# Splitting a down-projection weight over partitions: 13 rows each and a remainder on four load engines, instead of 12 rows and five small pieces

## The chip, the cores and the metric

The kernel runs on one core of a Trainium2 chip. The metric is device time in microseconds (us) of one execution. It reads about 95 MB from HBM once and does little arithmetic on each byte.

## The reference

One decode step for a batch of B = 2 with one token each, D = 512, all in float32. The output is the input plus an attention block plus a gated feed-forward block, both on the layer-normalised input:

```python
def _A_ref(x, k_cache, v_cache, wq, wo):     # Hq = 32 heads of Dh = 128, Hkv = 8
    W = min(4096, max(256, Sk // 4))         # 4096: the last W cached positions
    q = (x @ wq).reshape(B, Sq, Hq, Dh)...
    scores = einsum("bhqd,bhkd->bhqk", q, k) * (Dh ** -0.5)
    o = einsum("bhqk,bhkd->bhqd", softmax(scores), v)
    return o.reshape(B, Sq, Hq * Dh) @ wo    # wo: 4096 x 512

def _B_ref(x, W_gate, W_up, W_down):         # F = 1792
    gate = einsum("bsd,df->bsf", x, W_gate)
    up = einsum("bsd,df->bsf", x, W_up)
    gate = gate * (gate > 0)
    return einsum("bsf,fd->bsd", gate * up, W_down)   # W_down: 1792 x 512

xn = _layernorm(x)
return x + _A_ref(xn, ...) + _B_ref(xn, ...)
```

## The kernel before

All large transfers are issued by SP in program order into a pool `ring` of four buffers of 32 KB per partition, so a transfer is issued when the buffer four places earlier has been read. The order is: `wq` (two halves of 4 MB), `W_gate` and `W_up` (3.5 MB each), then for four groups of (key/value head quad, batch row) two `k` tiles and, one group later, two `v` tiles of 4 MB, then `W_down` (3.5 MB, `load_down`), then `wo` in two halves of 4 MB, the second cut into pieces of 8, 5, 2 and 1 rows per partition so that little is left to do when the last one lands.

PE runs in the order in which the code is written. After the query projection comes the gated unit: `g_ps` and `u_ps` hold gate and up in a layout of four groups of 32 partitions (each group takes a quarter of the 1792 columns, 448), one element per column. ScalarE and VectorE make `hh` = relu(gate) * up from them, and small matmuls against columns of the identity (`ht_ps`) turn `hh` so that the feed-forward index runs over partitions; `hT` holds the result. Then, for each `k` tile, 64 blocks are transposed (`pk`, copied to `kT` by VectorE and ScalarE in turn), multiplied by the queries (`scores`), and, one group later, the softmax weights are multiplied with `v` (`values`, `o`). At the end, `project` adds `hT` times `W_down` and the attention output `oT` times `wo` into one accumulator `y_ps`, four matmuls for each row of the weight in a partition.

Row k of a partition of `W_down` has to meet the element of `hT` at the same partition and k. With 1792 = 128 x 14 rows, a plain split would give 14 rows a partition. `load_down` uses another one: the 1792 rows are 32 runs of 56, and of each run the first 48 go to four partitions with 12 rows each (one transfer, 24 KB per partition), the last 8 to four partitions with two rows each. These remainders go in five small transfers, with 4 KB per partition: three of 8 runs (32 partitions each), and two of 4 runs (16 partitions each), the last into a tile of its own, `wx`. One part of the `W_down` tile is cleared by GpSimd first.

Of the kernel before, what the change touches and what calls it, by code (L numbers as in the profile page):

```python
# [9 lines left out]
F32 = mybir.dt.float32  # L10
AF = mybir.ActivationFunctionType
ALU = mybir.AluOpType
# [8 lines left out]
def kernel(  # L21
# [12 lines left out]
    nc = tc.nc  # L34
    P = 128
    B, _, D = x.shape
# [3 lines left out]
    F = w_gate.shape[1]  # L40
    W = min(4096, max(256, SK // 4))
    KC = D // P
# [3 lines left out]
    Q = 4  # L46
# [6 lines left out]
    PK = P // 2  # L53
    J = W // PK
    FB = F // P
    FQ = F // Q
    assert (B, REP, DH, S1, J) == (2, 4, P, 2, 64)

    const = ctx.enter_context(tc.tile_pool(name="const", bufs=1))
    ring = ctx.enter_context(tc.tile_pool(name="ring", bufs=RING))  # L60
    ktp = ctx.enter_context(tc.tile_pool(name="ktp", bufs=2))
    work = ctx.enter_context(tc.tile_pool(name="work", bufs=2))
    ps_kt = ctx.enter_context(tc.tile_pool(name="ps_kt", bufs=3, space=PSUM))
    ps_s = ctx.enter_context(tc.tile_pool(name="ps_s", bufs=1, space=PSUM))
    ps_1 = ctx.enter_context(tc.tile_pool(name="ps_1", bufs=1, space=PSUM))
# [13 lines left out]
    def load_ff(w, name):  # L79
        return load(name, w.rearrange("(p k) f -> p k f", p=P), [P, KC, F])  # L80
# [3 lines left out]

    FR = F // 32
    FM = FB - 2
    assert FR == 4 * FM + 8
    wx = const.tile([16, 2, D], F32, name="wx")  # L90

    def load_down():
        t = ring.tile([P, FM + 4, D], F32, name="wd", tag="ring")
        runs = w_down.rearrange("(i x) e -> i x e", i=32)
        main = bass.AP(
            tensor=w_down.tensor, offset=w_down.offset, ap=[[FR * D, 32], [FM * D, 4], [1, FM * D]]
        )
        nc.sync.dma_start(t[:, 0:FM].rearrange("p k e -> p (k e)"), main)
        nc.gpsimd.memset(t[32:64, FM + 2:], 0.0)
        for i, n, dst in (  # L100
            (0, 8, t[0:32, FM:FM + 2]), (8, 8, t[32:64, FM:FM + 2]), (16, 8, t[0:32, FM + 2:]),
            (24, 4, t[32:48, FM + 2:]), (28, 4, wx),
        ):
            src = runs[i:i + n, 4 * FM:, :].rearrange("i (y s) e -> i y (s e)", s=2)
            nc.sync.dma_start(dst.rearrange("p s e -> p (s e)"), src)
        return t

    def load_kv(cache, name, g, a):
        r, b = divmod(g, B)
        base = cache[b, r * C + 2 * a, SK - W:SK, :]  # L110
        run = J * DH
        src = bass.AP(
            tensor=cache.tensor, offset=base.offset, ap=[[run, PK], [SK * DH, 2], [1, run]]
        )
        return load(f"{name}{g}_{a}", src, [P, run])
# [15 lines left out]
    ident = const.tile([P, P], F32, name="ident")  # L131
# [7 lines left out]
    eps_t = const.tile([32, 1], F32, name="eps_t")  # L139
    nc.vector.memset(eps_t, EPS)  # L140

    hT = const.tile([P, FM + 6, B, 16], F32, name="hT")
    nc.gpsimd.memset(hT, 0.0)
    oT = const.tile([P, R, NJ, B, 16], F32, name="oT")
    nc.gpsimd.memset(oT, 0.0)
    xsel = const.tile([B, B, 16], F32, name="xsel")
# [53 lines left out]
    for kc in range(KC):  # L200
        m, k = divmod(kc, 2)
        for o, cols in ((0, xn.rearrange("r (m p k) -> r m k p", m=2, k=2)[:, m, k]), (1, xn.rearrange("r (p k) -> r k p", k=KC)[:, kc])):
            nc.tensor.matmul(xt_ps[:, o, kc, :], cols, rep.rearrange("r s b -> r (s b)"), start=True, stop=True)  # L203
    xnT = const.tile([P, 2, KC, 32], F32, name="xnT")
# [4 lines left out]
    for kc in range(KC):  # L209
        for r in range(R):  # L210
            for c in range(C):
                n = r * C + c
                nc.tensor.matmul(  # L213
                    q_ps[r][32 * c:32 * c + 32, :], xnT[:, 0, kc, :], wqt[kc // 2][:, kc % 2, n * 512:(n + 1) * 512],
                    start=(kc == 0), stop=(kc == KC - 1),
                )
    gw = load_ff(w_gate, "wg")
    uw = load_ff(w_up, "wu")
    for r in range(R):
        qs = work.tile([P, 512], F32, name=f"qs{r}", tag="qs")  # L220
# [6 lines left out]
        for b in range(B):  # L227
            dst = qz[:, r * B + b].rearrange("p (a s h k) -> p a s h k", a=NP, s=S1, h=2)
# [3 lines left out]
                )  # L232


    g_ps = ps_kt.tile([P, FQ], F32, name="g_ps", tag="kt")
    u_ps = ps_kt.tile([P, FQ], F32, name="u_ps", tag="kt")
    for dst, wt in ((g_ps, gw), (u_ps, uw)):
        for kc in range(KC):
            for c in range(Q):
                nc.tensor.matmul(  # L240
                    dst[32 * c:32 * c + 32, :], xnT[:, 1, kc, :], wt[:, kc, c * FQ:(c + 1) * FQ],
                    start=(kc == 0), stop=(kc == KC - 1),
                )
    gs = work.tile([P, FQ], F32, name="gs", tag="qs")
    nc.scalar.copy(gs, g_ps)
    gr = work.tile([P, FQ], F32, name="gr", tag="qs")
    nc.vector.scalar_tensor_tensor(gr, gs, 0.0, gs, op0=ALU.is_gt, op1=ALU.mult)
    hh = work.tile([P, FB, 32], F32, name="hh", tag="qs")
    gv = gr.rearrange("p (i x) -> p i x", i=8)
    uv = u_ps.rearrange("p (i x) -> p i x", i=8)  # L250
    nc.vector.tensor_tensor(
        hh[:, 0:FM].rearrange("p k (i y) -> p i y k", i=8), gv[:, :, 0:4 * FM].rearrange("p i (y k) -> p i y k", y=4),
        uv[:, :, 0:4 * FM].rearrange("p i (y k) -> p i y k", y=4), op=ALU.mult,
    )
    nc.vector.tensor_tensor(
        hh[:, FM:].rearrange("p s (i y) -> p i y s", i=8),
        gv[:, :, 4 * FM:].rearrange("p i (y s) -> p i y s", s=2),
        uv[:, :, 4 * FM:].rearrange("p i (y s) -> p i y s", s=2), op=ALU.mult,
    )
    ht_ps = ps_1.tile([P, FM + 6, B], F32, name="ht_ps", tag="misc")  # L260
    for k in range(FM):
        for c in range(Q):
            nc.tensor.matmul(
                ht_ps[32 * c:32 * c + 32, k], hh[:, k], ident[:, 32 * c:32 * c + B], start=True, stop=True
            )
    for s in range(2):
        for c, p0, k, cols in ((0, 0, 0, (0, 32)), (1, 32, 0, (0, 32)), (2, 0, 2, (0, 32)), (3, 32, 2, (0, 16)), (3, 0, 4, (16, 32))):
            nc.tensor.matmul(
                ht_ps[p0:p0 + cols[1] - cols[0], FM + k + s], hh[:, FM + s, cols[0]:cols[1]],
                ident[:, 32 * c:32 * c + B], start=True, stop=True,  # L270
            )
    for n, lo, hi in ((P, 0, FM), (64, FM, FM + 2)):
        nc.vector.tensor_copy(hT[0:n, lo:hi, :, 0], ht_ps[0:n, lo:hi])
    for p0, n, lo, hi in ((0, 32, FM + 2, FM + 4), (32, 16, FM + 2, FM + 4), (0, 16, FM + 4, FM + 6)):
        nc.vector.tensor_copy(hT[p0:p0 + n, lo:hi, :, 0], ht_ps[p0:p0 + n, lo:hi])

# [115 lines left out]
    def finish(g):  # L394
        r, b = divmod(g, B)
        if b == 0:
            osb[r] = const.tile([HR, B, P], F32, name=f"osb{r}")
        nc.vector.tensor_scalar(osb[r][:, b], oa[g], rls[g], 2.0, op0=ALU.mult, op1=ALU.mult)

    def spread_heads(r):  # L400
        op = ps_1.tile([P, NJ, B], F32, name=f"op{r}", tag="misc")
        for e in range(NE):
            nc.tensor.matmul(  # L403
                op, spread[:, e].rearrange("h k e -> h (k e)"),
                osb[r][:, :, e * NJ:(e + 1) * NJ].rearrange("h b j -> h j b"),
                start=(e == 0), stop=(e == NE - 1),
            )
        nc.vector.tensor_copy(oT[:, r, :, :, 0], op)
# [33 lines left out]
    g = NG - 1  # L442
    scores(*pend.pop())
    vin = [load_kv(v_cache, "v", g, a) for a in range(NP)]
    dw = load_down()
    for _ in softmax(g):
        pass

# [9 lines left out]
    def project(lhsT, w, stop):  # L458
        for e in range(Q):
            nc.tensor.matmul(  # L460
                y_ps[32 * e:32 * e + 17, :], lhsT.rearrange("p b s -> p (b s)")[:, 0:17],
                w[:, e * P:(e + 1) * P], start=False, stop=stop,
            )
# [2 lines left out]
        values(g, a, vin[a])  # L466
        gather(g, a)
    finish(g)
    for k in range(FM + 4):
        n = P if k < FM else 64  # L470
        project(hT[0:n, k], dw[0:n, k], False)
    for k in range(2):
        project(hT[0:16, FM + 4 + k], wx[:, k], False)
    spread_heads(R - 1)
    for r, cuts in ((0, (0, NJ)), (1, (0, 8, 13, 15, NJ))):
        wt = ring.tile([P, NJ, D], F32, name=f"wo{r}", tag="ring")
# [35 lines left out]
```

## Time and profile before

| | us |
|---|---|
| median of 3 runs | 231.94 (231.25 to 231.98) |
| profiled execution: its own span, first to last instruction | 230.3 |
| what lies around the span, against the median | 1.6 |
| PE busy in the span | 184.4 (80%) |
| VectorE busy | 67.1 (29%) |
| ScalarE busy | 48.4 (21%) |
| GpSimd busy | 6.6 (3%) |
| bytes moved by DMA | 95.15 MB in 3936 packets, 413 GB/s on average |

The page divides the span into 40 slices and shows in tenths how busy each engine was in each; the DMA row there is the mean over the core's 16 DMA engines. A transfer that SP issues is split by partitions over some or all of these 16 engines, each of which works through its own share in order; a transfer has landed when the slowest has written its share. In the queue rows, q1 is the queue of SP's transfers, and q8 brings the program's own instructions. The chain of waits is followed back from the last instruction, and shows at each step what the step had waited for.

### The profile page before, as it was taken

Reading aid. Unit: us, or ns where it says so; the run is one execution under the profiler, and the core shown is the slowest. Engines: PE = TensorE matmul, PEld = TensorE weight load, DVE = VectorE, ACT = ScalarE, POOL = GpSimd, SP = SyncE. Lnnn points to the kernel's source line nnn. Section 1 sums busy time; section 2 is a strip of 40 time slices with the busy share of each in tenths; the row PEclk is TensorE's granted clock in tenths of the full one; section 3 lists DMA queues with packets and bytes.
Section 4 is the critical chain, followed back from the end, with each engine's and each line's share of the span. In section 5 each row is a group of like instructions: output and inputs, shape, how many; then the busy total and the mean of one; then the engine's idle time right before and its main releaser. Section 6 shows DMA issues by size and latency. Waiting matters only on the chain.

```text
span 230.3 us, 4141 instructions
## 1 busy us (share of the span) xinstructions
PE 184.4 (80%) x1872; PEld 112.3 (49%) x1872; DVE 67.1 (29%) x136; ACT 48.4 (21%) x81; POOL 6.6 (3%) x23
## 2 busy tenths in 40 slices
PE   0295960849999889998999799589999974979593
PEld 0251220239666573664584565338566522148482
DVE  0500021023544462441472341147234123010000
ACT  2000100003444461540252331025133102000000
POOL 8100000000000000000000000000000100000000
PEclk9999799575999999999999999979999997699889
DMA  7999999999999999999999999999999999999980
GB/s 274 450 433 411 443 423 455 410 427 447 438 407 433 448 427 404 441 438 427 413 450 425 433 421 435 433 433 427 430 438 430 415 438 421 423 451 404 422 328 21
DMA packets 3936, 95.15 MB, mean 413 GB/s; under 512 B 454, under 2 KB 462, under 8 KB 848
## 3 DMA queue, kind: packets, MB, share of 16 engines
q1 hardware_dynamic: 3916, 94.90, 96.3%
q8 instruction: 14, 0.23, 0.4%
q14 instruction: 2, 0.02, 0.0%
q10 hardware_dynamic: 4, 0.00, 0.0%
HBM read 94.90 MB, written 0.00 MB: 412 GB/s over the span
## 4 chain that ended last, share of the span: by engine, by line
PE 46%; DMA 44%; DVE 4%; POOL 2%; ACT 1%; issue 1%; POOLq 0%
DMA k<-in_A_k_cache_dram 25%; PE pk L296 23%; DMA wd<-in_B_W_down_dram 11%; PE s L309 9%; DMA wo<-in_A_wo_dram 8%; PE o L373 5%; PE q_ps L213 3%; PE xt_ps L203 2%; PE pp L353 1%; DVE kT L285 1%; ACT p L342 1%; PE y_ps L460 1%; PE op L403 1%; PE oa L389 1%; POOL spread L155 1%
## 5 line engine op out<-in xcount | busy, mean ns | idle before, releaser
L296 PE MATMUL pk<-ident,k 128*128 128x128 f32 x512 | 68.1, 287 | 4.9 <-DMA k<-in_A_k_cache_dram 4.9
L296 PEld LDWEIGHTS pk<-ident,k 128*128 128x128 f32 x512 | 57.9, 146 | 19.8 <-issue 15.6
L285 DVE COPY kT<-pk 128x512 f32<-128x512 f32 x64 | 44.2, 691 | 50.6 <-PE pk L296 40.6
L285 ACT COPY kT<-pk 128x512 f32<-128x512 f32 x64 | 37.5, 586 | 81.8 <-PE pk L296 81.8
L309 PE MATMUL s<-kT,qz 128*32 128x512 f32 x256 | 31.9, 615 | 0.0
L373 PE MATMUL o<-v,pt 128*32 128x512 f32 x256 | 31.9, 631 | 0.0
L373 PEld LDWEIGHTS o<-v,pt 128*32 128x32 f32 x256 | 11.2, 116 | 15.3 <-issue 10.6
L309 PEld LDWEIGHTS s<-kT,qz 128*32 128x32 f32 x256 | 7.2, 112 | 12.8 <-issue 12.4
L213 PE MATMUL q_ps<-wq,xnT 128*32 128x512 f32 x64 | 10.9, 844 | 3.1 <-DMA wq<-in_A_wq_dram 2.6
L460 PE MATMUL y_ps<-wo,oT 128*17 128x128 f32 x256 | 9.3, 308 | 3.6 <-DMA wo<-in_A_wo_dram 3.6
L203 PE MATMUL xt_ps<-rep,xn 2*128 2x32 f32 x16 | 3.7, 400 | 10.2 <-DVE xn L197 10.2
L389 PE MATMUL oa<-on,pick 128*16 128x128 f32 x64 | 8.3, 273 | 4.1 <-DVE on L285 3.3
L285 DVE COPY on<-o 128x512 f32<-128x512 f32 x4 | 2.8, 692 | 29.9 <-PE o L373 29.9
L389 PEld LDWEIGHTS oa<-on,pick 128*16 128x16 f32 x64 | 5.8, 97 | 11.1 <-DVE on L285 7.0
L240 PE MATMUL u_ps<-wu,xnT 128*32 128x448 f32 x32 | 5.6, 870 | 6.8 <-DMA wu<-in_B_W_up_dram 6.8
L460 PEld LDWEIGHTS y_ps<-wo,oT 128*17 128x17 f32 x256 | 7.6, 111 | 5.1 <-DMA wo<-in_A_wo_dram 4.5
L203 PEld LDWEIGHTS xt_ps<-rep,xn 2*128 2x128 f32 x16 | 3.6, 319 | 10.2 <-issue 10.2
L285 ACT COPY on<-o 128x512 f32<-128x512 f32 x4 | 2.3, 586 | 26.6 <-PE o L373 26.6
L213 PEld LDWEIGHTS q_ps<-wq,xnT 128*32 128x32 f32 x64 | 2.5, 150 | 10.8 <-issue 6.6
L353 PE MATMUL pp<-ident,p 128*128 128x128 f32 x32 | 5.2, 295 | 2.4 <-ACT p L342 1.5
L342 ACT ACTIVATE p<-s,nm 128x1024 f32<-128x1024 f32 x4 | 4.5, 1116 | 12.5 <-DVE nm L337 12.5
L240 PEld LDWEIGHTS u_ps<-wu,xnT 128*32 128x32 f32 x32 | 1.4, 168 | 10.9 <-DMA wu<-in_B_W_up_dram 7.6
(77 smaller groups left out, 67.6 us busy)
## 6 DMA issues: line engine op xcount, KB each, us to landing
k<-in_A_k_cache_dram SPq DMA_DIRECT2D x8, 4096.0 KB, 26.5
v<-in_A_v_cache_dram SPq DMA_DIRECT2D x8, 4096.0 KB, 26.5
wq<-in_A_wq_dram SPq DMA_DIRECT2D x2, 4096.0 KB
wo<-in_A_wo_dram SPq DMA_DIRECT2D x1, 4096.0 KB, 28.3
wg<-in_B_W_gate_dram SPq DMA_DIRECT2D x1, 3584.0 KB, 29.7
wu<-in_B_W_up_dram SPq DMA_DIRECT2D x1, 3584.0 KB, 39.3
wd<-in_B_W_down_dram SPq DMA_DIRECT2D x1, 3072.0 KB, 26.4
wo<-in_A_wo_dram SPq DMA_DIRECT2D x1, 2048.0 KB, 20.6
```

The costliest lines, as they stand in the source:

```text
L155: nc.gpsimd.tensor_copy(spread[:, e, :, e], ident[0:HR, 0:HR])
L203: nc.tensor.matmul(xt_ps[:, o, kc, :], cols, rep.rearrange("r s b -> r (s b)"), start=True, stop=True)
L213: nc.tensor.matmul(q_ps[r][32 * c:32 * c + 32, :], xnT[:, 0, kc, :], wqt[kc // 2][:, kc % 2, n * 512:(n + 1) * 512], start=(kc == 0), stop ...
L240: nc.tensor.matmul(dst[32 * c:32 * c + 32, :], xnT[:, 1, kc, :], wt[:, kc, c * FQ:(c + 1) * FQ], start=(kc == 0), stop=(kc == KC - 1),)
L285: (nc.vector.tensor_copy if turn[0] % 2 else nc.scalar.copy)(dst, src)
L296: nc.tensor.transpose(pk[:, u * P:(u + 1) * P], kt_in[:, j * P:(j + 1) * P], ident)
L309: nc.tensor.matmul(ss[g][32 * q:32 * q + 32, :], qz[:, g, 32 * n:32 * n + 32], kt[:, h, q * 512:(q + 1) * 512], start=(a == 0 and s1 == 0 ...
L342: nc.scalar.activation(p, both, AF.Exp, bias=nm, scale=SCALE, accum_out=l)
L353: nc.tensor.transpose(pp[:, u], pv[:, lo:lo + P], ident)
L373: nc.tensor.matmul(o[32 * q:32 * q + 32, :], pts[g][:, jh, n].rearrange("p u k -> p (u k)"), v[:, lo:lo + 512], start=(s1 == 0 and jh == 0 ...
L389: nc.tensor.matmul(oa[g], pick[:, u, 8 - 8 * a:24 - 8 * a], ons[a][:, u], start=(a == 0 and u == 0), stop=(a == NP - 1 and u == 3),)
L460: nc.tensor.matmul(y_ps[32 * e:32 * e + 17, :], lhsT.rearrange("p b s -> p (b s)")[:, 0:17], w[:, e * P:(e + 1) * P], start=False, stop=stop,)
```

## The change

`W_down` is split differently. The first 128 x 13 = 1664 rows are one plain transfer, 13 consecutive rows (26 KB) for each partition. The last 128 rows go to a tile `wx` of their own, four rows (8 KB) in each of 32 partitions, in two transfers of 16 partitions. The source of each is written as a 4 x 4 pattern of such blocks, with the outer dimension of 4 (`KX`) first. `wx` has a buffer of the pool of the transposed keys (`ktp`, two buffers); it is cleared by GpSimd over 64 partitions before the transfers write into partitions 0 to 15 and 32 to 47. `LEFT` is 0, so the code for it does nothing.

On SP the transfers of `W_down` and their neighbours, before (the last `v` tile, `W_down` in `wd` and `wx`, and the start of `wo`):

```order
L71 DMA v_1_1525<-in_A_v_cache_dram 128x1x8192
L98 DMA wd<-in_B_W_down_dram 128x1x6144
L105 DMA wd<-in_B_W_down_dram 32x1x1024 x3
L105 DMA wd<-in_B_W_down_dram 16x1x1024
L105 DMA wx<-in_B_W_down_dram 16x1x1024
L478 DMA wo_1706<-in_A_wo_dram 128x8192
L478 DMA wo_1772<-in_A_wo_dram 128x4096
```

The same place after the change:

```order
L70 DMA v_1_1534<-in_A_v_cache_dram 128x1x8192
L99 DMA wd<-in_B_W_down_dram 128x6656
L108 DMA wx<-in_B_W_down_dram 16x1x2048 x2
L497 DMA wo_1709<-in_A_wo_dram 128x8192
L497 DMA wo_1775<-in_A_wo_dram 128x4096
```

Five small transfers become two of twice the width; the main one grows by 512 elements a partition, and nothing changes its place.

The gated unit follows that split: the first 1664 columns go through the four groups of 32 partitions (416 each), and the last 128 are computed apart, in `x_ps` on 32 partitions, with operations of their own up to `hx` and the last rows of `hT`. On PE, from the gate product to the first transposed key block (`pk`), before:

```order
L240 MATMUL g_ps<-wg,xnT 32x448 x16
L240 MATMUL u_ps<-wu,xnT 32x448 x16
L263 MATMUL ht_ps<-ident,hh 32x2 x48
L268 MATMUL ht_ps<-ident,hh 32x2 x3
L268 MATMUL ht_ps<-ident,hh 16x2 x2
L268 MATMUL ht_ps<-ident,hh 32x2 x3
L268 MATMUL ht_ps<-ident,hh 16x2 x2
L296 MATMUL pk_0_0_0_321<-ident,k_0_318 128x128 x4
```

And after:

```order
L249 MATMUL g_ps<-wg,xnT 32x416 x16
L254 MATMUL x_ps<-wg,xnT 32x128 x4
L249 MATMUL u_ps<-wu,xnT 32x416 x16
L254 MATMUL x_ps<-wu,xnT 32x128 x4
L285 MATMUL ht_ps<-ident,hh 32x2 x52
L290 MATMUL ht_ps<-ident,hx 64x2 x4
L315 MATMUL pk_0_0_0_330<-ident,k_0_327 128x128 x4
```

Eight matmuls with 128 columns are new, four of them between the up product and the transposing; those become 56 instead of 58. At the end of the program 13 + 4 rows of `W_down` are projected instead of 12 + 4 + 2.

The diff, without the asserts and the code for `LEFT`:

```diff
+    FM = 13
+    KX = 4
+    LEFT = 0
+    FX = F - P * FM
+    RX = (FX - 8 * LEFT) // (8 * KX)
+    SX = RX + (LEFT > 0)
+    MQ = P * FM // Q
...
     def load_down():
-        t = ring.tile([P, FM + 4, D], F32, name="wd", tag="ring")
-        runs = w_down.rearrange("(i x) e -> i x e", i=32)
-        main = bass.AP(
-            tensor=w_down.tensor, offset=w_down.offset, ap=[[FR * D, 32], [FM * D, 4], [1, FM * D]]
-        )
-        nc.sync.dma_start(t[:, 0:FM].rearrange("p k e -> p (k e)"), main)
-        nc.gpsimd.memset(t[32:64, FM + 2:], 0.0)
-        for i, n, dst in (
-            (0, 8, t[0:32, FM:FM + 2]), (8, 8, t[32:64, FM:FM + 2]), (16, 8, t[0:32, FM + 2:]),
-            (24, 4, t[32:48, FM + 2:]), (28, 4, wx),
-        ):
-            src = runs[i:i + n, 4 * FM:, :].rearrange("i (y s) e -> i y (s e)", s=2)
-            nc.sync.dma_start(dst.rearrange("p s e -> p (s e)"), src)
-        return t
+        t = ring.tile([P, FM, D], F32, name="wd", tag="ring")
+        wx = ktp.tile([P, SX, D], F32, name="wx", tag="kT")
+        nc.gpsimd.memset(wx[0:64], 0.0)
+        nc.sync.dma_start(
+            t.rearrange("p k e -> p (k e)"), w_down[0:P * FM, :].rearrange("(p k) e -> p (k e)", p=P)
+        )
+        row = P * FM
+        for b in range(2):
+            src = bass.AP(
+                tensor=w_down.tensor, offset=w_down.offset + row * D,
+                ap=[[RX * D, KX], [KX * RX * D, 4], [1, RX * D]],
+            )
+            nc.sync.dma_start(wx[32 * b:32 * b + 4 * KX, 0:RX].rearrange("p k e -> p (k e)"), src)
+            row += 4 * KX * RX
...
+    hx = const.tile([32, SX, 64], F32, name="hx")
+    nc.gpsimd.memset(hx, 0.0)
...
+        for kc in range(KC):
+            nc.tensor.matmul(
+                x_ps[:, h], xnT[:, 1, kc, :], wt[:, kc, Q * MQ:], start=(kc == 0), stop=(kc == KC - 1)
+            )
...
+    gx = work.tile([32, 2, FX], F32, name="gx", tag="qs")
+    nc.scalar.copy(gx[:, 0], x_ps[:, 0])
+    nc.vector.scalar_tensor_tensor(gx[:, 1], gx[:, 0], 0.0, gx[:, 0], op0=ALU.is_gt, op1=ALU.mult)
+    part = 4 * KX * RX
+    for b in range(2):
+        g_in, u_in = (
+            a[:, b * part:(b + 1) * part].rearrange("p (j e s) -> p e j s", j=4, e=KX) for a in (gx[:, 1], x_ps[:, 1])
+        )
+        nc.vector.tensor_tensor(
+            hx[:, 0:RX, 32 * b:32 * b + 4 * KX].rearrange("p s (e j) -> p e j s", j=4), g_in, u_in, op=ALU.mult
+        )
...
-    for k in range(FM + 4):
-        n = P if k < FM else 64
-        project(hT[0:n, k], dw[0:n, k], False)
-    for k in range(2):
-        project(hT[0:16, FM + 4 + k], wx[:, k], False)
+    for k in range(FM):
+        project(hT[:, k], dw[:, k], False)
+    for k in range(SX):
+        n = 64 if k < RX else 32
+        project(hT[0:n, FM + k], wx[0:n, k], False)
```

More of the change, by code (lines that the diff above doesn't have):

```diff
@@ L55 @@
     FB = F // P
-    FQ = F // Q
     assert (B, REP, DH, S1, J) == (2, 4, P, 2, 64)
@@ L80, in load_ff @@
         return load(name, w.rearrange("(p k) f -> p k f", p=P), [P, KC, F])
[L87 to L90, printed above, removed]
-    def load_down():
-        t = ring.tile([P, FM + 4, D], F32, name="wd", tag="ring")
-        runs = w_down.rearrange("(i x) e -> i x e", i=32)
-        main = bass.AP(
-            tensor=w_down.tensor, offset=w_down.offset, ap=[[FR * D, 32], [FM * D, 4], [1, FM * D]]
-        )
-        nc.sync.dma_start(t[:, 0:FM].rearrange("p k e -> p (k e)"), main)
-        nc.gpsimd.memset(t[32:64, FM + 2:], 0.0)
-        for i, n, dst in (
-            (0, 8, t[0:32, FM:FM + 2]), (8, 8, t[32:64, FM:FM + 2]), (16, 8, t[0:32, FM + 2:]),
-            (24, 4, t[32:48, FM + 2:]), (28, 4, wx),
-        ):
-            src = runs[i:i + n, 4 * FM:, :].rearrange("i (y s) e -> i y (s e)", s=2)
-            nc.sync.dma_start(dst.rearrange("p s e -> p (s e)"), src)
-        return t
+    FM = 13
[5 more added lines that the diff above has]
+    MQ = P * FM // Q
+    assert 8 * KX * RX + 8 * LEFT == FX
+    def load_down():
+        t = ring.tile([P, FM, D], F32, name="wd", tag="ring")
[3 more added lines that the diff above has]
+            t.rearrange("p k e -> p (k e)"), w_down[0:P * FM, :].rearrange("(p k) e -> p (k e)", p=P)
+        )
+        row = P * FM
[6 more added lines that the diff above has]
+            row += 4 * KX * RX
+        for i in range(LEFT):
+            nc.sync.dma_start(wx[i:32:4, RX], w_down[row + 8 * i:row + 8 * i + 8, :])
+        return t, wx
     def load_kv(cache, name, g, a):
@@ L140 @@
     nc.vector.memset(eps_t, EPS)
-    hT = const.tile([P, FM + 6, B, 16], F32, name="hT")
+    hT = const.tile([P, FM + SX, B, 16], F32, name="hT")
     nc.gpsimd.memset(hT, 0.0)
+    hx = const.tile([32, SX, 64], F32, name="hx")
+    nc.gpsimd.memset(hx, 0.0)
     oT = const.tile([P, R, NJ, B, 16], F32, name="oT")
@@ L232 @@
                 )
-    g_ps = ps_kt.tile([P, FQ], F32, name="g_ps", tag="kt")
-    u_ps = ps_kt.tile([P, FQ], F32, name="u_ps", tag="kt")
-    for dst, wt in ((g_ps, gw), (u_ps, uw)):
+    g_ps = ps_kt.tile([P, MQ], F32, name="g_ps", tag="kt")
+    u_ps = ps_kt.tile([P, MQ], F32, name="u_ps", tag="kt")
+    x_ps = ps_1.tile([32, 2, FX], F32, name="x_ps", tag="o0")
+    for h, dst, wt in ((0, g_ps, gw), (1, u_ps, uw)):
         for kc in range(KC):
@@ L240 @@
                 nc.tensor.matmul(
-                    dst[32 * c:32 * c + 32, :], xnT[:, 1, kc, :], wt[:, kc, c * FQ:(c + 1) * FQ],
+                    dst[32 * c:32 * c + 32, :], xnT[:, 1, kc, :], wt[:, kc, c * MQ:(c + 1) * MQ],
                     start=(kc == 0), stop=(kc == KC - 1),
                 )
-    gs = work.tile([P, FQ], F32, name="gs", tag="qs")
+        for kc in range(KC):
+            nc.tensor.matmul(
+                x_ps[:, h], xnT[:, 1, kc, :], wt[:, kc, Q * MQ:], start=(kc == 0), stop=(kc == KC - 1)
+            )
@@ L245 @@
+    gs = work.tile([P, MQ], F32, name="gs", tag="qs")
     nc.scalar.copy(gs, g_ps)
-    gr = work.tile([P, FQ], F32, name="gr", tag="qs")
+    gr = work.tile([P, MQ], F32, name="gr", tag="qs")
     nc.vector.scalar_tensor_tensor(gr, gs, 0.0, gs, op0=ALU.is_gt, op1=ALU.mult)
-    hh = work.tile([P, FB, 32], F32, name="hh", tag="qs")
-    gv = gr.rearrange("p (i x) -> p i x", i=8)
-    uv = u_ps.rearrange("p (i x) -> p i x", i=8)
+    hh = work.tile([P, FM, 32], F32, name="hh", tag="qs")
     nc.vector.tensor_tensor(
-        hh[:, 0:FM].rearrange("p k (i y) -> p i y k", i=8), gv[:, :, 0:4 * FM].rearrange("p i (y k) -> p i y k", y=4),
-        uv[:, :, 0:4 * FM].rearrange("p i (y k) -> p i y k", y=4), op=ALU.mult,
-    )
@@ L255 @@
[L255 to L258, printed above, removed]
-    )
-    ht_ps = ps_1.tile([P, FM + 6, B], F32, name="ht_ps", tag="misc")
+        hh.rearrange("p k y -> p y k"), gr.rearrange("p (y k) -> p y k", k=FM),
+        u_ps.rearrange("p (y k) -> p y k", k=FM), op=ALU.mult,
+    )
+    gx = work.tile([32, 2, FX], F32, name="gx", tag="qs")
@@ L261 @@
+    for i in range(LEFT):
+        lo = 2 * part + 8 * i
+        nc.vector.tensor_tensor(
+            hx[:, RX, i:32:4], gx[:, 1, lo:lo + 8], x_ps[:, 1, lo:lo + 8], op=ALU.mult
+        )
+    ht_ps = ps_1.tile([P, FM + SX, B], F32, name="ht_ps", tag="misc")
     for k in range(FM):
@@ L265 @@
             )
[L266 to L275, printed above, removed]
+    for k in range(SX):
+        m = 64 if k < RX else 32
+        nc.tensor.matmul(ht_ps[0:m, FM + k], hx[:, k, 0:m], ident[0:32, 0:B], start=True, stop=True)
+    nc.vector.tensor_copy(hT[:, 0:FM, :, 0], ht_ps[:, 0:FM])
+    nc.vector.tensor_copy(hT[0:64, FM:FM + RX, :, 0], ht_ps[0:64, FM:FM + RX])
+    if LEFT:
+        nc.vector.tensor_copy(hT[0:32, FM + RX, :, 0], ht_ps[0:32, FM + RX])
     HW = W // S1
@@ L444 @@
     vin = [load_kv(v_cache, "v", g, a) for a in range(NP)]
-    dw = load_down()
+    dw, wx = load_down()
     for _ in softmax(g):
@@ L468 @@
     finish(g)
-    for k in range(FM + 4):
-        n = P if k < FM else 64
-        project(hT[0:n, k], dw[0:n, k], False)
-    for k in range(2):
-        project(hT[0:16, FM + 4 + k], wx[:, k], False)
+    for k in range(FM):
+        project(hT[:, k], dw[:, k], False)
+    for k in range(SX):
+        n = 64 if k < RX else 32
+        project(hT[0:n, FM + k], wx[0:n, k], False)
     spread_heads(R - 1)
```

## The prediction

> **What bounds the kernel now.** I read the page first: the slices, then the DMA queues, then the groups.
>
> ```profile
> span 230.3 us, 4141 instructions
> PE 184.4 (80%) x1872; PEld 112.3 (49%) x1872; DVE 67.1 (29%) x136; ACT 48.4 (21%) x81; POOL 6.6 (3%) x23
> ...
> DMA  7999999999999999999999999999999999999980
> ...
> q1 hardware_dynamic: 3916, 94.90, 96.3%
> q8 instruction: 14, 0.23, 0.4%
> ```
>
> The 16 DMA engines are over 90% busy in every slice but the first and the last two, while the busiest compute engine has a fifth of the span free. So the transfers are the limit. From the q1 row one engine moves a KB in 0.963 x 16 x 230.3 / 94,900 KB = 37.4 ns; this price is used below. The q8 row is the program's own instructions: 14 fetches of 16 KB, each 0.004 x 16 x 230.3 / 14 = 1.05 us of one engine's time.
>
> Next come the end of the chain of waits and the windows of its last microseconds; their last two columns are the busy share of the DMA engines and GB/s.
>
> ```profile
> 179.18 26.44 DMA wd<-in_B_W_down_dram
> 205.62 0.02 issue
> 205.64 19.32 DMA wo<-in_A_wo_dram
> 224.96 0.04 issue
> 225.00 1.88 PE y_ps L460 x56
> 226.88 0.01 issue
> 226.88 0.46 PE y_ps L460 x8
> 227.34 0.02 issue
> 227.37 0.29 DVE yo L482
> ```
>
> ```profile
> 220.00:221.00 1.00, 1.00 (x38) 0.96 (x32) 0.00 (x0) 0.00 (x0) 0.00 (x0) 0.86 0.94 391
> 221.00:222.00 1.00, 1.00 (x45) 1.00 (x40) 0.00 (x0) 0.00 (x0) 0.00 (x0) 1.00 0.91 379
> 222.00:223.00 1.00, 1.00 (x48) 1.00 (x41) 0.00 (x0) 0.00 (x0) 0.00 (x0) 1.00 0.79 320
> 223.00:224.00 1.00, 1.00 (x40) 0.75 (x28) 0.00 (x0) 0.00 (x0) 0.00 (x0) 1.00 0.64 254
> 224.00:225.00 1.00, 0.03 (x5) 0.00 (x1) 0.00 (x0) 0.00 (x0) 0.00 (x0) 1.00 0.35 139
> 225.00:226.00 1.00, 1.00 (x37) 1.00 (x40) 0.00 (x0) 0.00 (x0) 0.00 (x0) 1.00 0.14 55
> 226.00:227.00 1.00, 0.99 (x32) 0.47 (x25) 0.00 (x0) 0.00 (x0) 0.00 (x0) 1.00 0.03 10
> ```
>
> The DMA share sinks from 0.94 to nothing over five microseconds: the engines run dry one after another, and in 225 to 226 only 0.14 x 16 = 2.2 of them work on average. The last piece of `wo` waits for the last engine; from there 3.5 us of matmuls, copy and store end the kernel. What counts is the engine that is last, not the sum over engines.
>
> To see which one that is, I chained the packet records of q1: each packet begins within a few ns of another's end, so they fall into 16 rows, one for each engine, told apart by their count of 4 KB packets (only the small `w_down` pieces have those). My working, in page time:
>
> ```
> group  engines  4 KB packets   KB of w_down   end of the engine's last packet, us
> A      4        20             192 + 80       224.15 224.29 225.06 225.40
> B      4        12             192 + 48       222.88 222.93 226.10 226.35
> C      8        0              192            221.22 221.28 222.85 222.97 223.14 224.07 224.61 224.77
> ```
>
> That agrees with the issues:
>
> ```profile
> wd<-in_B_W_down_dram SPq DMA_DIRECT2D x1, 3072.0 KB, 26.4
> ...
> wd<-in_B_W_down_dram SPq DMA_DIRECT2D x3, 128.0 KB
> ...
> wd<-in_B_W_down_dram SPq DMA_DIRECT2D x1, 64.0 KB
> wx<-in_B_W_down_dram SPq DMA_DIRECT2D x1, 64.0 KB
> ```
>
> 3072 KB over 16 engines is 192 each. Three transfers of 128 KB, with an outer dimension of 8, go to A and B (16 KB, four packets each); the two of 64 KB, with one of 4, go to A alone. [...]
>
> Inside a group the ends differ by instruction fetches: a stretched packet and a gap of about 1.1 us follow each. Eight engines take them in turn, six of C and two of B: two each to two of B and three of C by the end, one each to three of C. The step is about 1.65 us (C: 221.25, 223.0, 224.5). The last engine, 226.35, is in B: 48 KB of small pieces plus two fetches.
>
> **The change, part by part.**
>
> *The main transfer* has 13 rows (26 KB) for each partition instead of 12. Each engine serves 8 partitions, so it gets 16 KB more: 16 x 37.4 ns = +0.60 us on all 16.
>
> *The small pieces.* 256 KB remain, in two transfers of 128 KB whose source has an outer dimension of 4: 64 KB on each of four engines, A if those are the four that carry the 64 KB pieces now. A: 64 instead of 80 KB, -0.60. B: none instead of 48, -1.80. C: none as before. The trace of before has no such 8 KB packets in q1; their price is bounded by bytes (37.4 ns a KB) and by two 4 KB packets at the pitch of group A in the chained records (155 ns each), 2.39 and 2.48 us for 64 KB. I take the first, as larger packets come at the price of the page. The four A engines' 80 KB took 3.1 us as chained, so the second end gives -0.6 too.
>
> Sum by group: A 0.0, B -1.2, C +0.6. New ends: A up to 225.40, B up to 226.35 - 1.20 = 225.15, C up to 224.77 + 0.60 = 225.37. The last engine would end at 225.40 instead of 226.35, **0.95 us earlier**, in a tie of A and C. All late pieces of `wo` shift alike, as each lands with the slowest engine, so the 3.5 us behind are kept.
>
> [...]
>
> *The issue of the transfers.*
>
> ```profile
> 179.08 1.92 PE L309 MATMUL s<-kT,qz 128*32 128x512 f32 x16
> 179.18 0.54 SPq L98 DMA_DIRECT2D wd<-in_B_W_down_dram  x1
> ...
> 179.26 0.94 POOL L99 MEMSET wd<- 32x1024 f32 x1 [172.89 <-PE pk L296]
> ...
> 179.77 2.98 SPq L105 DMA_DIRECT2D wd<-in_B_W_down_dram  x4
> ...
> 182.79 0.64 SPq L105 DMA_DIRECT2D wx<-in_B_W_down_dram  x1
> ...
> 188.66 0.33 SPq L478 DMA_DIRECT2D wo<-in_A_wo_dram  x1
> ```
>
> A new wait: `wx` now lies in a buffer of the transposed keys, whose last readers are the score matmuls that end at 181.0. GpSimd clears it after that; twice the columns of the 0.94 us memset are at most 1.9 us, so 182.9. SP holds both `wx` issues until then, and behind them the first `wo` issue. Two issues of 0.7 us end at 184.3; `wo` isn't issued before 188.66 now. Cover 4.4 us, cost 0. Beyond it the queue has a backlog: the main piece lands 26.4 us after its issue, of which 3072 KB / 16 x 37.4 ns = 7.2 us are its own.
>
> *The gated unit.*
>
> ```profile
> 41.41 5.57 PE L240 MATMUL u_ps<-wu,xnT 128*32 128x448 f32 x32 [6.75 <-DMA wu<-in_B_W_up_dram]
> ...
> 47.06 0.80 DVE L251 TENSOR_TENSOR hh<-gr,u_ps 128x384 f32<-128x384 f32 x1 [11.10 <-PE u_ps L240]
> 47.72 0.25 DVE L255 TENSOR_TENSOR hh<-gr,u_ps 128x64 f32<-128x64 f32 x1
> ...
> 51.22 5.14 PE L296 MATMUL pk<-ident,k 128*128 128x128 f32 x23 [2.02 <-DMA k<-in_A_k_cache_dram]
> ```
>
> ```profile
> L389 PE MATMUL oa<-on,pick 128*16 128x128 f32 x64 | 8.3, 273 | 4.1 <-DVE on L285 3.3
> ```
>
> The 16 matmuls for `u_ps` shrink from 448 to 416 columns, 7% of 5.57 = -0.4 us. Four with 128 columns follow (eight instructions). They all write the same 32 partitions; the nearest row in shape, `oa`, also of 128 columns into one place, takes 8.3 / 64 = 0.13 us for one: 1.0 us, and about twice that where PE runs at half clock, as the length of this stage suggests. The same four for the gate lie in PE's 6.75 us wait for `wu`. On VectorE two products of 1.05 us become one of about as much and a short chain on 32 partitions (a copy on ScalarE, three operations near the 0.25 us of the 64-element product), at most 1 us, in part beside the 52 transposing matmuls. So PE may come to the first `pk` matmul up to 2.7 us later, against 2.02 us that it waits there for `k`. Were 0.7 us left over, this would delay the release of `k` buffers, not the transfers: by the issue and landing times above, what is queued keeps the engines busy for 19 us (26.4 - 7.2). Likewise the clearing of `hx` on GpSimd at the start (below the 0.9 us of the memset above) delays only the start of PE, which then waits for weights. Cost 0. At the end 68 groups of four projecting matmuls replace 72; they stand before `wo` and aren't on the chain: 0.
>
> Sum: -0.95 us, with 0.1 either way for the unknown packets.
>
> **The rivals.**
>
> *The fetches fall otherwise (slower).* Where the instruction fetches land isn't set by the source, and the new program has other instructions. If two fell on group A, an undisturbed A engine (224.15) would get 2 x 1.65 us and end at 227.45; if one of the C engines that end at 224.77 got a third, it would end at 224.77 + 0.60 + 1.65 = 227.02. Both are later than 226.35, by 1.1 and 0.7: about 232.9 us. It decides as soon as an engine that ends above 224.7 gets one more. For it: C gets nearer to the edge by 0.6 us. Against it: the eight engines came in a fixed turn through the whole trace, and about as many instructions are fetched. Chance 0.15.
>
> *No change.* The end is A's after the change, and A gains nothing. If in the runs that are timed A already ends last (the lowest run, 231.25, is 0.7 below the median, about what B's lead over A's last is: 226.35 - 225.40), or if 8 KB and 26 KB packets cost A some 0.5 us more than by bytes, the time stays between 231.4 and 232.2. Chance 0.23.
>
> *The pieces go to other engines.* Were the 256 KB spread over all 16, each would get 16 KB of them: A would end at 225.40 - 1.80 = 223.60, B at 226.35 - 0.60 = 225.75, C at 224.77 + 1.20 = 225.97: 0.4 us gained. This is the rival in which the edit isn't what it says; the four 64 KB pieces now, on four engines with the same outer dimension, speak against it. Chance 0.05, about 231.6.
>
> **How the numbers follow.** The forecast has 0.57. The profiled span is 230.3 us, 1.6 us below the median of 231.94; what lies around the span is kept, so the span goes to 229.35 and the time to 231.94 - 0.95 = 230.99, rounded to 231.0. A measurement of this kernel can tell about 0.3% (0.7 us) from no change; the forecast lies 0.25 us beyond that, and its own spread (0.1 for the packets, some 0.3 for a median of runs that lie 0.7 apart) leaves part of it within. Range: from 230.5 (forecast less its spread) to 232.5, which takes in no change and the lower part of the slower rival. Faster by over 0.3%: three quarters of 0.57, and some of the lower edge of the no-change case, 0.50; within: 0.32; slower: 0.18, the rival's 0.15 and a little of the no-change case.
>
> **What would show it.** Right: in the windows of the tail the DMA share falls more steeply and reaches nothing about 1 us earlier; the first engines run dry 0.6 us later; the chained packets show 64 KB in 8 KB packets on four engines, none on the others; `wo` is issued no later than 188.7; the last `y_ps` group and the store shift by the same 0.95. Wrong: a DMA share below 0.9 before the tail (a starved queue), SP waiting for GpSimd past 188, more than the first `pk` delayed on PE; or a last engine of group C with three fetches, or of group A with one.

## The result, and the profile after

| | before | after |
|---|---|---|
| median of 21 runs each, us | 231.90 (231.04 to 232.13) | 231.44 (231.23 to 231.69) |
| span of the profiled execution, us | 230.3 | 229.5 |

The ratio of the times is 0.9983, with a 95% interval of 0.9976 to 0.9989: 0.46 us faster by the medians (0.3 to 0.6 by the interval), by 0.2%. The direction was forecast, and the time lies within the range; the gain is half of the 0.95 us that was forecast. The profiled execution of the change itself took 231.31 us, 1.8 more than its span. Of the executions here and below, three that lie far above all others (two of the kernel before at 256 us, one of the 4 KB kernel at 451) are left out of the ratios.

The head of its page, as of before: the slices, q1 and q8 are nearly the same, so the transfers are still the limit and the instruction fetches still 14.

```profile
span 229.5 us, 4147 instructions
...
DMA  7999999999999999999999999999999999999991
...
q1 hardware_dynamic: 3796, 94.90, 96.7%
q8 instruction: 14, 0.23, 0.4%
```

The windows of its tail (the last two columns are the DMA engines' busy share and GB/s) and the end of its chain:

```profile
221.00:222.00 1.00, 1.00 (x45) 0.92 (x37) 0.00 (x0) 0.00 (x0) 0.00 (x0) 1.00 0.99 406
222.00:223.00 1.00, 1.00 (x47) 1.00 (x39) 0.00 (x0) 0.00 (x0) 0.00 (x0) 1.00 0.75 309
223.00:224.00 1.00, 0.32 (x12) 0.04 (x3) 0.00 (x0) 0.00 (x0) 0.00 (x0) 1.00 0.71 274
224.00:225.00 1.00, 0.85 (x32) 0.85 (x36) 0.00 (x0) 0.00 (x0) 0.00 (x0) 1.00 0.50 195
225.00:226.00 1.00, 1.00 (x32) 0.50 (x24) 0.00 (x0) 0.00 (x0) 0.00 (x0) 1.00 0.13 49
226.00:227.00 1.00, 0.47 (x12) 0.13 (x8) 0.29 (x1) 0.00 (x0) 0.00 (x0) 1.00 0.00 0
```

```profile
201.59 22.51 DMA wo<-in_A_wo_dram
224.10 0.04 issue
224.15 1.91 PE y_ps L479 x56
226.06 0.02 issue
226.08 0.46 PE y_ps L479 x8
226.54 0.02 issue
226.56 0.29 DVE yo L501
```

The share is 0.99 in 221 to 222 (0.91 before) and 0.50 in 224 to 225 (0.35 before), but nothing is left after 226. More engines work up to near the end, and the end is earlier: the last group of `y_ps` begins at 226.08 instead of 226.88, by 0.80 us where the forecast had 0.95.

The chained packets say which engine is last. The table is my working from the packet records of two profiles of each kernel, here with the records of four bytes that close each engine's share of a transfer, which makes the rows unambiguous. `[2]`, `[1]` are instruction fetches that an engine got; no mark is none. The second pair of profiles comes from the experiments. After the change four engines (A) have eight packets of 8 KB each, 64 KB, and the others have none, so the pieces went where the edit says.

```
kernel          span   group: end of each engine's last packet, us
before          230.3  A 224.16 224.30 225.06 225.41    B 222.88 222.93 226.10[2] 226.36[2]
                       C 221.22 221.28 222.86[1] 222.97[1] 223.15[1] 224.07[2] 224.62[2] 224.77[2]
before again    229.4  A 224.38 224.44 224.95 225.47    B 223.03 223.05 224.52[1] 224.58[1]
                       C 221.19 221.28 222.69[1] 224.17[2] 224.40[2] 224.46[2] 224.57[2] 224.63[2]
after           229.5  A 224.61 224.68 225.10 225.57    B and C 221.95 222.01 222.20 222.63 223.52[1]
                       223.56[1] 223.65[1] 225.02[2] 225.24[2] 225.44[2] 225.44[2] 225.44[2]
after again     230.1  A 224.63 224.70 225.12 225.91    B and C 221.88 221.94 222.01 222.27 223.70[1]
                       223.82[1] 223.93[1] 225.10[2] 225.14[2] 225.31[2] 225.42[2] 225.42[2]
```

The terms of the forecast can be read in it: from the first packet of `W_down` to its last packet of all, an engine of A took 30.07 us (30.09 before), one of C whose fetches all lie earlier 27.56 (26.89), and one of the 12 without a fetch 27.56, where an engine of B without one took 28.79: 0.0, +0.7 and -1.2 us, against 0.0, +0.6 and -1.2 forecast.

### The profile page after: what moved, and what is told of

Its sections match the earlier page's. It is cut to its first block, busy times and chain, and to the rows that moved or that the text cites. A ratio compares the mean times of both kernels' runs of the same rounds, so it can differ in the third digit from the quotient of the medians.

```text
span 229.5 us, 4147 instructions
## 1 busy us (share of the span) xinstructions
PE 183.6 (80%) x1876; PEld 114.8 (50%) x1876; DVE 67.3 (29%) x135; ACT 48.6 (21%) x82; POOL 7.7 (3%) x24
## 4 chain that ended last, share of the span: by engine, by line
PE 53%; DMA 34%; DVE 5%; POOL 2%; ACT 2%; issue 1%; SPq 0%; POOLq 0%
DMA k<-in_A_k_cache_dram 25%; PE pk L315 23%; PE s L328 11%; DMA wo<-in_A_wo_dram 10%; PE o L392 9%; PE q_ps L221 2%; PE pp L372 2%; PE xt_ps L211 2%; ACT p L361 2%; PE oa L408 2%; DVE kT L304 1%; PE y_ps L479 1%; PE op L422 1%; DVE on L304 1%; POOL spread L163 1%
## 5 line engine op out<-in xcount | busy, mean ns | idle before, releaser
L221 PE MATMUL q_ps<-wq,xnT 128*32 128x512 f32 x64 | 9.2, 727 | 3.3 <-DMA wq<-in_A_wq_dram 2.8
L98 POOL MEMSET wx<- 64x2048 f32 x1 | 1.8, 1804 | 174.5 <-PE s L328 174.5
L249 PE MATMUL g_ps<-wg,xnT 128*32 128x416 f32 x32 | 4.7, 752 | 2.6 <-DMA wg<-in_B_W_gate_dram 2.6
```

Of the source, the lines that this page charges most:

```text
L221: nc.tensor.matmul(q_ps[r][32 * c:32 * c + 32, :], xnT[:, 0, kc, :], wqt[kc // 2][:, kc % 2, n * 512:(n + 1) * 512], start=(kc == 0), stop ...
L249: nc.tensor.matmul(dst[32 * c:32 * c + 32, :], xnT[:, 1, kc, :], wt[:, kc, c * MQ:(c + 1) * MQ], start=(kc == 0), stop=(kc == KC - 1),)
```

## The experiments

**The kernel before, profiled again.** No edit.

> The kernel before once more, for a second profile of it. Theory of the last engine: if the instruction fetches fall twice on an engine of B, that engine ends at 226.1 to 226.4 and the span is about 230.1 to 230.3; if they fall twice on engines of C alone, A is last at 225.4 and the span is 229.4. If the fetches always take the same turn, the profile repeats the first one, 226.35.

Its span is 229.4, and the share in 225 to 226 is 0.03 instead of 0.14, with nothing after 226:

```profile
span 229.4 us, 4141 instructions
...
225.00:226.00 1.00, 0.99 (x36) 0.47 (x27) 0.00 (x0) 0.00 (x0) 0.00 (x0) 1.00 0.03 10
226.00:227.00 1.00, 0.38 (x8) 0.10 (x8) 0.29 (x1) 0.00 (x0) 0.00 (x0) 1.00 0.00 0
```

In the table, both B engines that fetch got one fetch each in this execution and five of C got two; the last engine is of A, at 225.47. So the same program takes its fetches in a turn that begins elsewhere from one execution to the next, and its end moves by 0.9 us with it. Its times agree: in the four sets of this kernel 18 of 82 lie between 230.9 and 231.5 us, the others at 231.7 and above, most near 231.9.

**The change, again.** No edit.

> The changed kernel once more, for a second profile and a second set of times. Theory of the last engine: the kernel ends with whichever of the 16 DMA engines is last; with the change groups A (64 KB of small pieces) and C (two instruction fetches) are level (225.56 and 225.44 in the profile), and B with two fetches would end at about 225.2, so whichever engines the fetches fall on, the end is 225.4 to 225.6: times in one cluster, 231.2 to 231.7, while the kernel before shows two, near 231.2 and 231.9, by whether an engine of B got two fetches. Rival (fewer and larger transfers saved the time): one cluster for both kernels.

12 runs: 231.47 median, 231.13 to 231.84, without a gap between two groups, as forecast (though wider than the 231.2 to 231.7 forecast); ratio 0.9987 (0.9973 to 1.0). The profile is the longest of these runs: A ends at 225.91 and sets the end, 0.35 later than in the first profile; the range forecast, 225.4 to 225.6, was too narrow. It is the engine of A that also takes an 8 KB fetch of another queue (q14) near 80 us; in all four rows for A in the table the last entry is that engine.

**The remainder on eight engines.**

```diff
-    KX = 4
+    KX = 8
```

> The remainder goes to eight engines (KX 8: two transfers of 32 partitions with 4 KB each) instead of four. Theory of the last engine: A gets 32 KB less (-1.2 us: at most 224.4), B 32 KB more (+1.2: 224.7 with one fetch, 226.4 with two), C as in the changed kernel (225.4). So 231.3 in executions in which no engine of B gets two fetches and 232.2 to 232.3 in the others, two clusters 0.9 us apart, as the kernel before has. Rival (fewer and larger transfers): two transfers as in the changed kernel, packets of 4 KB instead of 8: at most 0.2 us slower, one cluster.

The median is 232.13, ratio to the kernel before 1.0008 (0.9994 to 1.0022). Of 12 runs three took 231.1 to 231.4 and nine 232.0 to 232.3: the two groups, 0.9 us apart, where forecast. The profile is one of the second:

```profile
span 230.3 us, 4107 instructions
...
225.00:226.00 1.00, 1.00 (x48) 0.99 (x40) 0.00 (x0) 0.00 (x0) 0.00 (x0) 1.00 0.21 80
226.00:227.00 1.00, 0.97 (x40) 0.56 (x28) 0.00 (x0) 0.00 (x0) 0.00 (x0) 1.00 0.02 8
```

Chained, the two engines that are last (226.13 and 226.31) have 4 KB packets and two fetches each; forecast was 226.4. A transfer count of two, the same as in the change, doesn't keep its time.

**The remainder on two engines.**

```diff
-    KX = 4
+    KX = 2
```

> The remainder goes to two engines (KX 2: two transfers of 8 partitions with 16 KB each): 128 KB on each of them. Theory of the last engine: two engines of A get 64 KB more, 2.4 us; in the profile A ended at 224.6, 224.7, 225.1 and 225.6, so the last ends at 227.0 to 228.0, 1.5 to 2.4 us later than with four: 232.9 to 233.9. Rival (fewer and larger transfers): same number, larger packets, so no slower than the changed kernel, 231.4.

233.40 us, ratio 1.0083 (1.006 to 1.0106). Two engines end at 226.87 and 227.66, all others by 225.30. The windows show the two alone: 0.12 x 16 = 1.9 engines.

```profile
225.00:226.00 1.00, 0.18 (x8) 0.00 (x0) 0.00 (x0) 0.00 (x0) 0.00 (x0) 1.00 0.13 53
226.00:227.00 1.00, 0.78 (x29) 0.78 (x32) 0.00 (x0) 0.00 (x0) 0.00 (x0) 1.00 0.12 45
227.00:228.00 1.00, 1.00 (x36) 0.58 (x26) 0.00 (x0) 0.00 (x0) 0.00 (x0) 1.00 0.12 33
```

**The same bytes in 4 KB packets.**

```diff
-            src = bass.AP(... ap=[[RX * D, KX], [KX * RX * D, 4], [1, RX * D]])
-            nc.sync.dma_start(wx[32 * b:32 * b + 4 * KX, 0:RX]..., src)
+            for c in range(2):
+                src = bass.AP(... + c * (RX // 2) * D, ap=[[RX * D, KX], [KX * RX * D, 4], [1, RX // 2 * D]])
+                dst = wx[32 * b:32 * b + 4 * KX, c * (RX // 2):(c + 1) * (RX // 2)]
+                nc.sync.dma_start(dst..., src)
```

> The changed kernel with each of the two remainder transfers cut into two with 4 KB packets; the bytes on each engine are the same. Theory of the last engine: 16 packets at 155 ns for 8 at 312 on A, no change: 231.4 (+0.1 at most). Rival (fewer and larger transfers saved the time): four small transfers of 4 KB packets for the five of the kernel before bring back its time, 231.8 to 231.9.

231.35 us, ratio 0.9977 (0.9968 to 0.9986): the time of the change, with four small transfers instead of two. The size and number of the small packets isn't what was gained.

**The gated unit's extra matmuls four times.**

```diff
-        for kc in range(KC):
+        for kc in [k for _ in range(4) for k in range(KC)]:
             nc.tensor.matmul(x_ps[:, h], ...)
```

> The changed kernel with the matmuls of the remainder's gate and up products run four times over, with the same result. Theory of the last engine: 3 to 6 us more on PE between the up product and the first transposed key block delay the release of buffers, not the transfers, which are queued some 19 us deep: 231.4, no change. Rival (the gated unit's remainder is on the path, and took back half of the forecast gain): its 1 us becomes 4, so 234 or more.

231.41 us, ratio 0.9979 (0.997 to 0.9987): no change. In the timeline the matmuls of `x_ps` take 3.55 us instead of 1.04, and PE still waits 1.57 us for `k` afterwards, against 4.06 in the change. The cover was larger than forecast, as `u_ps` takes 3.00 us in both instead of the 5.57 of before. That was luck and not the change: the granted clock was 1.00 there (41 to 44 us) and 0.57 before (41 to 47), and in the second profile of the change `u_ps` took 4.69 us and PE waited 2.37 for `k`. The change first, then the four-fold matmuls:

```profile
43.87 1.04 PE L254 MATMUL x_ps<-wu,xnT 128*32 128x128 f32 x8
...
50.87 1.51 PE L315 MATMUL pk<-ident,k 128*128 128x128 f32 x6 [4.06 <-DMA k<-in_A_k_cache_dram]
```

```profile
41.28 3.00 PE L249 MATMUL u_ps<-wu,xnT 128*32 128x416 f32 x32 [1.75 <-DMA wu<-in_B_W_up_dram]
44.10 3.55 PE L254 MATMUL x_ps<-wu,xnT 128*32 128x128 f32 x31
...
51.09 5.17 PE L315 MATMUL pk<-ident,k 128*128 128x128 f32 x43 [1.57 <-DMA k<-in_A_k_cache_dram]
```

**The remainder on all 16 engines.** The blocks of each transfer are taken in order, and the layout of `hx` follows.

```diff
-            src = bass.AP(... ap=[[RX * D, KX], [KX * RX * D, 4], [1, RX * D]])
+            src = w_down[row:row + 4 * KX * RX, :].rearrange("(p k) e -> p (k e)", k=RX)
```

> The remainder's 128 rows go to all 16 engines (the source of each transfer is 16 consecutive blocks of 8 KB). Theory of the last engine: 16 KB of it for each engine, so A -1.8 us (223.8), B +0.6 (225.8 with two fetches), C +0.6 (226.0 with two fetches, which some C engine has in every execution): 0.5 us slower than the changed kernel, 231.9 to 232.0, about the time of the kernel before, in one cluster. Rival (use of all 16 engines is best): 1 to 2 us faster than the changed kernel at these transfers, or equal.

235.21 us, ratio 1.0153 (1.0129 to 1.0176): 3.3 us slower than the 231.9 forecast, and not for the last engine's bytes. All engines end late, the earliest at 226.1, because packets are stretched from 202 on: in the packet records those of 26 KB take up to 1.9 us (0.99 until then), those of 32 KB up to 3.0 (1.22 in the change). In the windows, which count a packet where it begins, the busy share is above 1 while the GB/s fall by a third, and then to 86. From 202 to 210 the mean is 234 GB/s, in the change 438: 8 us at 53% lose 3.7 us, so this stretch accounts for the excess.

```profile
200.00:202.00 2.00, 2.00 (x16) 0.39 (x8) 0.00 (x0) 0.00 (x0) 0.00 (x0) 0.74 1.01 426
202.00:204.00 2.00, 1.23 (x16) 1.03 (x19) 0.00 (x0) 0.59 (x1) 0.00 (x0) 1.00 1.18 293
204.00:206.00 2.00, 2.00 (x24) 1.06 (x20) 0.00 (x0) 0.00 (x0) 0.00 (x0) 1.00 1.20 275
206.00:208.00 2.00, 1.25 (x12) 0.23 (x4) 0.66 (x1) 0.00 (x0) 0.00 (x0) 1.00 1.27 280
208.00:210.00 2.00, 1.91 (x54) 1.79 (x55) 0.37 (x2) 0.00 (x0) 0.00 (x0) 1.00 0.38 86
```

From the outer dimension of 16 I took each transfer to go to 16 engines, which then write into the same 16 partitions, one each; the one of 4 put eight 8 KB packets on each of four engines in the change. There an engine of A writes four partitions of each transfer. I took these to be ones that it also serves in the large transfers; no trace shows which partitions an engine writes. Three more kernels tell how far the cost follows the partitions.

**Fourteen plain rows.** One transfer of 28 KB a partition; the `wx` transfers, `x_ps`, `gx` and `hx` are gone.

```diff
-    FM = 13
+    FM = 14
...
-        wx = ktp.tile([P, SX, D], F32, name="wx", tag="kT")
...
```

> All of W_down in one plain transfer of 14 rows for each partition; no remainder, and nothing of the gated unit apart. Theory of the last engine: 224 KB on each engine, so against the changed kernel A gets 48 KB less (-1.8 us, 223.8 at most), B and C 16 KB more (+0.6); some engine of B or C with two fetches ends at 225.8 to 226.1 in every execution: 231.9 to 232.0. Each engine writes only its own eight partitions here, so if the 3.3 us that the 16-engine remainder cost beyond its forecast come from sixteen engines writing the same 16 partitions, they are absent. Rival (the parts that are computed and moved apart cost time): faster than the changed kernel, 231.0 or less. Rival (16 engines at the remainder are slow whatever the partitions): 235.

231.69 us, ratio to the kernel before 0.9994 (0.9985 to 1.0004). One group of runs, 231.57 to 231.92; the last engine ends at 225.93, with two fetches (forecast 225.8 to 226.1). The time is 0.2 below what I expected: the forecast added 0.5 to the change's median, as if C set the change's end, but there it is A, 0.1 to 0.5 us later, in each of the four profiles with 64 KB on A. The simplest split is slower than the change by some 0.2 us (and than the 4 KB packets, timed in the same set, by 0.3) although it saves matmuls and two transfers, and needs no remainder.

**The remainder over 128 partitions, and over 64.** One transfer each, 2 KB or 4 KB a partition, with the gated products laid out to suit.

```diff
...
+        nc.sync.dma_start(wx[0:128, 0:1]..., w_down[P * FM:, :].rearrange("(p k) e -> p (k e)", k=1))
...
```

> [...] If the 16-engine remainder cost 3.3 us more than forecast because sixteen engines wrote into the same 16 partitions: none of that here, and by the last engine (A -1.8, B and C +0.6) 226.0, as with 14 plain rows: 231.7 to 231.9. If a small transfer over 16 engines is slow in itself: 233 or more.

> [...] If crowding of engines on the same partitions is what costs: two engines where the 16-engine remainder had four, so some stretching of packets around 203 to 205 us, less than a third of the 3.3 us: 231.9 to 232.8. If it doesn't cost at two: 231.7 to 231.9.

128 partitions: 231.65 us, ratio 0.9995 (0.9983 to 1.0006), as with plain rows. 64 partitions: 234.34 us, ratio 1.0117 (1.0086 to 1.0147). So the small transfer over 16 engines cost nothing beyond its bytes here when it went to all 128 partitions (the last engine ends at 225.68; 226.0 was forecast by bytes), and 2.7 us more (234.34 against 231.65) when it went to 64, far more than I had expected of half the crowding. That engines crowd each other on the same partitions fits both and the 16-engine kernel, but is my guess and not shown: the traces show that packets are stretched, not where they wait. The windows of the two, 64 partitions first:

```profile
202.00:204.00 2.00, 2.00 (x23) 1.40 (x27) 0.00 (x0) 0.00 (x0) 0.00 (x0) 1.00 1.21 382
204.00:206.00 2.00, 2.00 (x24) 0.85 (x16) 0.00 (x0) 0.00 (x0) 0.00 (x0) 1.00 1.02 302
206.00:208.00 2.00, 1.17 (x14) 0.69 (x14) 0.69 (x1) 0.00 (x0) 0.00 (x0) 1.00 1.07 303
```

```profile
202.00:204.00 2.00, 2.00 (x23) 1.35 (x25) 0.00 (x0) 0.00 (x0) 0.00 (x0) 1.00 1.02 425
204.00:206.00 2.00, 2.00 (x21) 0.70 (x12) 0.00 (x0) 0.00 (x0) 0.00 (x0) 1.00 1.15 487
206.00:208.00 2.00, 1.17 (x20) 0.90 (x22) 0.69 (x1) 0.00 (x0) 0.00 (x0) 1.00 0.95 410
```

No version beat the change by more than can be told: 4 KB packets (231.35) and four-fold matmuls (231.41) are level with it.

## Why the prediction was right, and why the gain was half

*Right: the engine that is last sets the end, and the groups.* Four experiments that move bytes between engines and little else came out where the sum by groups puts them: eight engines 226.31 (226.4 forecast), two engines 227.66 (227.0 to 228.0), plain rows 225.93 (225.8 to 226.1), 4 KB packets 225.63 (as in the change, 225.6). Two did not, the 16-engine remainder into 32 partitions (229.68, not 226.0) and into 64 (227.97): the sum prices a KB alike wherever it is written. The two engines against four that the forecast for 64 partitions sets beside each other are in no run; what the runs showed in their place is 2.0 us beyond plain rows there (227.97 against 225.93) and 3.8 for 32 partitions. All terms of the change itself were within 0.1 us.

*Right: what was costed at nothing.* The new wait on GpSimd is there and free:

```profile
179.10 0.33 SPq L99 DMA_DIRECT2D wd<-in_B_W_down_dram  x1
...
181.07 1.80 POOL L98 MEMSET wx<- 64x2048 f32 x1 [174.47 <-PE s L328]
...
182.90 1.52 SPq L108 DMA_DIRECT2D wx<-in_B_W_down_dram  x2
185.29 0.34 SPq L497 DMA_DIRECT2D wo<-in_A_wo_dram  x1
```

The issues end at 184.4 (184.3 forecast), and `wo` follows at 185.3, earlier than before: the 188.66 of before wasn't its earliest time. The gated unit is free too, by the four-fold matmuls. What follows the last engine is 3.9 us (230.3 - 226.36), not 3.5, but as long after the change (229.5 - 225.57), so it drops out.

*Wrong: the step from one profile to the median.* "What lies around the span is kept, so ... the time to 231.94 - 0.95" took the profiled execution for a typical one. Three things were missed there; the first and the third make the 0.45 us between 231.44 and the 230.99 forecast.

First, what lies around the span is 1.8 us, not 1.6 (231.31 against 229.5 in one and the same execution). So the profiled execution of before took about 232.1 and was 0.2 slower than the median.

Second, the turn of the fetches. I had taken its place as fixed ("came in a fixed turn through the whole trace") and put its moving into the slower rival. The order of engines is fixed, as far as the two profiles of before tell (the places of B in it differ by a shift of four), but not where in it an execution begins. When no B engine gets two fetches, A is last already, and the change gains nothing. The second profile of before shows one such execution; by the times they are about a fifth, with spans of 229.1 to 229.6, where the change has 229.3 to 230.1. This is the no-change rival, and it was true of some executions rather than of all. It moves the median little: without that fifth, the median of before would be 231.93 instead of 231.90. The slower rival fell on one point: in the six profiles in which the four engines of A can be told apart, A got none of these fetches, and no engine more than two.

Third, A ended later than forecast. The median span of 21 runs is 229.6, where the forecast had 229.35, with A and C level at 225.4. In all four profiles with 64 KB on each engine of A (the change twice, the 4 KB packets, the four-fold matmuls) the same engine of A is last, at 225.57 to 225.91, and no other engine ends after 225.47. Its bytes cost what was forecast, 0.0; but it began `W_down` at 195.50 to 195.84, before the change at 195.32 and 195.39. So it was late before the transfers that were changed, and why is open. That leaves 230.1 - 229.6 = 0.5 us between a usual execution of before and one after, as measured.

*Luck: the range.* It reached from 230.5 to 232.5 and took in no change, so that the time lies in it says little. The prediction took 0.3% as the least that can be told and preferred a larger gain (0.50) to one within it (0.32); the 0.2% measured is within it, and 231.44 also lies at the edge of the no-change rival's 231.4 to 232.2. It can be told from no change because each kernel ran 21 times. What shows the mechanism is the packets and the experiments, not the time.

## What to carry to other kernels

Where transfers are the limit, count bytes for each DMA engine and not in total, and look at the busy share of the tail: a slope instead of an edge (0.94 to 0.14 in five us before) came here from engines that ended between 221.22 and 226.36, and small transfers on four engines alone put the last end at 225.57 in the first profile of the change. A profile is one execution; before a sum is made against it, see how it stands to the runs, and whether something that isn't in the source moves from execution to execution. Once several engines are level, the next gain has to come off all of them.

## What the runs showed of the hardware that I had not expected

*Instruction fetches slowed single engines.* A 16 KB fetch cost its engine about 1.55 us (a packet stretched by 0.5 us and a gap of 1.05), where the bytes alone would take 0.6 (16 x 37.4 ns, an estimate from the price of the page before). In the two profiles of each kernel eight of the 16 engines took them, and in the second profile of before the turn began at another engine. In this kernel, which its transfers limit, the cost shows: 2 x 1.55 = 3.1 us for an engine that gets two (B before: 226.10 and 226.36, where the two without a fetch end at 222.88 and 222.93).

*The same bytes from 16 engines cost more on fewer partitions.* 256 KB into two sets of 16 partitions put the last engine's end 3.8 us later than plain rows (229.68 against 225.93), and into 64 partitions 2.0 (227.97), while 128 partitions cost nothing (225.68). The packets of the large transfers beside them were stretched too, between 202 and 210 us (those of 26 KB up to 1.9 us in the 16-engine kernel, 0.99 in the change). The change writes the same 32 partitions as the first of these, from four engines, and its packets aren't stretched (8 KB in 0.31 us, 32 KB in 1.22). Why fewer partitions cost more, no run shows.
